# Sliding-window attention with two MLPs: sinks inside each key tile, and one value tile shared by both query blocks of a unit

## The chip, the cores and the metric

The kernel runs on one core of a Trainium2 chip. The metric is the device time of one execution in microseconds (us). The engines are PE (TensorE; its weight loads are listed apart as PEld), DVE (VectorE), ACT (ScalarE), POOL (GpSimd) and SP, which here only issues DMAs.

## The reference: what is computed

```python
def _attn_ref(q, k, v, n_sink, window):            # q, k, v: [2, 8, 768, 64]
    scores = (1 / sqrt(64)) * (q @ k^T)
    keep = (pos_k < n_sink) | (0 <= pos_q - pos_k < window)     # n_sink 4, window 128
    scores = where(keep, scores, -1e9); a = exp(scores - max); a = a / (sum(a) + 1e-9)
    return a @ v
x = attention, heads side by side                   # [1536, 512]
x = elu(x @ w_in) @ w_out                           # [512, 2048], [2048, 512]
x = prelu(x @ w2_in, alpha) @ w2_out                # the same sizes
```

All inputs and the output are float32.

## The kernel before

**Attention.** A *unit* is the work of four heads on 128 queries: two head pairs (e = 0, 1), each of two heads (f = 0, 1). There are 24 units, x0 to x23 by the number of their output tile. Four of them (p = 0) hold the first 128 positions and have less work. The 128 queries of a unit are two blocks of 64 (j = 0, 1). Block 0 sees 128 keys of the tile before and the first 64 of its own; block 1 sees the last 64 of the tile before and all 128 of its own. Each also sees six sink columns, which the launch copies between the tiles, so a row of scores is 198 wide (`WMAX` = 128 + 6 + 64).

A unit passes these stages, each on one line of the code:

- `qk` (L766): eight score products on PE, K = 64 rows, 198 columns;
- `s` (L781): mask and row maximum on DVE; `s` (L789): exp and row sum on ACT; `st` (L799, L800): one over the sum on DVE; `s` (L817): the scaling on POOL;
- `t` (L837): sixteen transposes on PE; `pt` (L852): two copies out of PSUM, each on ACT or DVE as the planner chooses;
- `x` (L879): the value products on PE. For a unit with p > 0 each block has a full tile of 128 keys (kind "t") and an edge tile of 64 keys and 6 sinks (kind "e"), so 2 blocks x 2 tiles x 2 pairs x 2 heads = 16 products of 64 columns;
- `xh` (L893) on ACT and `xl` (L898) on DVE: the result split in a high and a low part.

Both full tiles differ: block 0 uses the 128 keys before the unit, block 1 the unit's own 128.

**MLPs.** Every product is done as three fp32r products of 128x128 weights with 512 columns (high x high, high x low, low x high), all on L983. `h` tiles are the first layer, `o` tiles the second; h0_0_3 is round 0, tokens 0 to 511, chunk 3. A *group* is the three products of one 128-row slice; four groups fill one h or o tile. Weights come as raw words and are decoded in eight steps on ACT, DVE and POOL (L438 to L460). An h tile goes through ACT (L1004, L1011), DVE (L1016), a copy `gh` on ACT or POOL (L1024) and a subtraction `gl` on DVE or POOL (L1027) before an o tile can use it.

**Order.** A planner (`class Plan`) places every step on an engine's queue with costs that are written in the code (800 ns for the `x` step of a unit with p > 0), and the engines then run these queues in order. Where it sees PE idle for more than 700 ns, it writes products that nobody reads into the queue (`busy`, L422), one for each 128 ns over that. `BANKS` lets at most three MLP tiles be open in PSUM in the planner's books. Loads of keys and values lie in one field of SBUF (`acc`, `more`), and a load is placed where the units that used that space have given it back.

Of the kernel before, what the change touches and what calls it, by code (L numbers as in the profile page):

```python
# [15 lines left out]
AF = mybir.ActivationFunctionType  # L16
# [3 lines left out]
B, H, S, D = 2, 8, 768, 64  # L20
NT, DM, DFF = B * S, H * D, 2048
P = 128
# [6 lines left out]


WIN, SINK, QB = 128, 6, 64
NPAIR = S // P
HP = H // 2

# [40 lines left out]
def key_columns(lo, hi):  # L75

    cols, scored = [], {}
    if lo:  # L80
        cols += range(lo * P - P, lo * P)
    for p in range(lo, hi):
        n = len(cols)
        if p:
            cols += [-1 - i for i in range(SINK)]
            scored[p] = (n - P, P + SINK + QB), (n - QB, QB + SINK + P)
        else:
            scored[p] = (0, QB), (0, P)
        cols += range(p * P, p * P + P)
    return cols, scored  # L90


# [8 lines left out]
SPAN, NCH, CR, VTILE, _cols = [], [], [], {}, []  # L101
for _r, (_lo, _hi) in enumerate(VRANGE):
    _sinks = [-1 - i for i in range(SINK)]
    _edge = [c for p in range(max(_lo, 1), _hi) for c in (*range(p * P - QB, p * P), *_sinks, *_sinks, *range(p * P, p * P + QB))]
    for _kind, _more, _high in (("t", [*range(_lo * P, _hi * P)], P), ("e", _edge, QB + SINK)):
        if _more:
            VTILE[_kind, _r] = len(SPAN), sum(NCH) * 2 * D, len(_more) // _high
            SPAN.append((len(_cols), len(_more)))
            NCH.append(len(_more) // _high)
            CR.append(_high)  # L110
            _cols += _more
KCOLS.append(_cols)
WMAX = P + SINK + QB
KTOT = [len(c) for c in KCOLS]

RUNS = [
    [(0, QB, 0)], [(0, P, -QB)], [(0, P, -P), (P, SINK, None), (P + SINK, QB, 0)],
    [(0, P, -P), (P, SINK, None), (P + SINK, QB, 0)], [(0, QB, -P), (QB, SINK, None), (QB + SINK, P, -QB)],  # L120
]
SINKS = [0, 0, 0, P, QB]
MW = [c + n for c, n, _ in (runs[-1] for runs in RUNS)]


def mask_of(p, j):
# [167 lines left out]
def attention_mlp2(  # L294
# [13 lines left out]
    nc = tc.nc  # L308
# [45 lines left out]
    def v_of(kind, b, hp, p):  # L354
        r = next(r for r, (lo, hi) in enumerate(VRANGE) if lo <= p < hi)
        return (kind, b, r, hp), p - (VRANGE[r][0] if kind == "t" else max(VRANGE[r][0], 1))
# [33 lines left out]
    for i, most in enumerate((SINK, 0, WIN, 0)):  # L390
# [7 lines left out]
        out=flag_i, in0=int1[:, 2:3].bitcast(U32), scalar=0.5, in1=flag_m, op0=ALU.is_ge, op1=ALU.mult  # L398
# [245 lines left out]
    for m in range(2):  # L644
        o = FIRST + sum(MW[:m])
# [5 lines left out]
    def fast_path():  # L651
# [35 lines left out]
        needs_v, first_v = {}, {}  # L687
        for i, (g, p) in enumerate(units):
            b, z, hp = sgs[g]
            needs_v[i] = [v_of("t", b, hp, p)[0]] + ([v_of("t", b, hp, p - 1)[0], v_of("e", b, hp, p)[0]] if p else [])  # L690
            for v in needs_v[i]:
                first_v.setdefault(v, i)
        uses_v = {v: sum(x.count(v) for x in needs_v.values()) for v in first_v}
# [55 lines left out]
        for i, (g, p) in enumerate(units):  # L749
            b, z, hp = sgs[g]  # L750
            nk, nq = KTOT[z], QTOT[z]
            tiles = {}
# [23 lines left out]
            for j, (_, w) in enumerate(SCORED[z][p]):  # L776
                m = mask_of(p, j)
                for e in range(2):

                    def least(e_, tiles=tiles, j=j, e=e, w=w, m=m):  # L780
                        nc.vector.tensor_tensor_reduce(  # L781
                            out=tiles["s"][:, j, e, :w], in0=tiles["qk", e][:, j * WMAX : j * WMAX + w],
                            in1=masks[m], scale=-SCALE, scalar=3.0e38, op0=ALU.add, op1=ALU.min,
                            accum_out=tiles["st"][:, 0, j, e : e + 1],
                        )

                    def power(e_, tiles=tiles, j=j, e=e, w=w):
                        s, st = tiles["s"], tiles["st"]
                        nc.scalar.activation(  # L789
                            s[:, j, e, :w], s[:, j, e, :w], AF.Exp, bias=st[:, 0, j, e : e + 1], scale=-1.0,  # L790
                            accum_out=st[:, 1, j, e : e + 1],
                        )

                    op = plan.add({"DVE": 75.0 + 1.06 * w}, least, deps=[sc, ready[m]], frees=[hq[e]], rank=i)
                    exps.append(plan.add({"ACT": 290.0 + 0.8 * w}, power, deps=[op], rank=i))

            def shares(e_, tiles=tiles):
# [7 lines left out]

            parts = (
                [[(1, 0, 0, QB)], [(0, 1, 0, P)]] if p == 0 else
                [[(0, 0, 0, P), (1, 0, P, QB + SINK)], [(1, 1, 0, QB + SINK), (0, 1, QB + SINK, P)]]
            )
            high_ = [P, QB if p == 0 else QB + SINK]  # L810
            ns_ = []
            for j, (_, w) in enumerate(SCORED[z][p]):
                for e in range(2):

                    def normal(e_, tiles=tiles, j=j, e=e, w=w):
                        s, st = tiles["s"], tiles["st"]
                        nc.gpsimd.tensor_scalar(  # L817
                            out=s[:, j, e, :w], in0=s[:, j, e, :w], scalar1=st[:, 3, j, e : e + 1], scalar2=1.0,
                            op0=ALU.mult, op1=ALU.mult,
                        )  # L820

                    ns_.append(plan.add({"POOL": 250.0 + 0.8 * w}, normal, deps=[share], rank=i, lock=True))


            def turned(e_, i=i, p=p, tiles=tiles, ht=ht, parts=parts):
                s = tiles["s"].rearrange("p j e w -> p (j e w)")
                for f in range(2):
                    tiles["t", f] = bank(f"t{i}_{f}", ht[f].slot)
                for j in range(2):
                    for a, _, c0, r in parts[j]:  # L830
                        r = min(r, QB) if p == 0 and a else P
                        for e in range(2):
                            o = (a * 4 + j * 2 + e) * QB
                            for f in range(2):
                                at_ = slice(f * QB, f * QB + QB)
                                r0 = (j * 2 + e) * WMAX + c0
                                nc.tensor.transpose(tiles["t", f][:r, o : o + QB], s[at_, r0 : r0 + r], ident[at_, at_])  # L837

            turns = plan.add(
# [7 lines left out]
            for f in range(2):  # L847
# [6 lines left out]
                n = sum(hi - lo for _, lo, hi in cuts_)  # L854
# [4 lines left out]
            def values(e_, i=i, p=p, b=b, hp=hp, tiles=tiles, hx=hx):  # L859
                px = tiles["x"] = bank(f"x{i}", hx.slot)  # L860

                def v(kind, p, n=0):
                    key, at_ = v_of(kind, b, hp, p)
                    return tiles_v[key][:, :, at_ * (1 if kind == "t" else 2) + n]

                if p == 0:
                    uses_ = [[(1, v("t", 0), QB)], [(0, v("t", 0), P)]]
                else:
                    uses_ = [
                        [(0, v("t", p - 1), P), (1, v("e", p, 1), QB + SINK)],  # L870
                        [(1, v("e", p), QB + SINK), (0, v("t", p), P)],
                    ]
                for j in range(2):
                    for e in range(2):
                        o = (e * 2 + j) * QB
                        for n, (a, vt, r) in enumerate(uses_[j]):
                            q0 = (a * 4 + j * 2 + e) * QB
                            for f in range(2):
                                nc.tensor.matmul(  # L879
                                    px[f * D : f * D + D, o : o + QB], vt[:r, e, f * D : f * D + D],  # L880
                                    tiles["p", f][:r, q0 : q0 + QB],
                                    start=(n == 0), stop=(n == len(uses_[j]) - 1),
                                )

            va = taken[i] = plan.add(
                {"PE": sum(len(x) for x in parts) * 4 * 50.0}, values,
                deps=copied + [land_v[v] for v in needs_v[i]],
                takes=[(kinds["tx"], 1, hx)], frees=hv + [hold_v[v] for v in needs_v[i]], rank=i - 3.0, kind="v",
            )
            c0, o = b * S + p * P, 2 * P  # L890
# [62 lines left out]
        for n, (kind, k, t, x) in enumerate(PIECES):  # L953
            m, r = divmod(k, NR)
            c0, nt = TOK[t]
            rank, op, hold, tiles = 100.0 + n, None, Hold(2 if kind == "f" else 1), {}
            for j in range(FG):
                if kind == "f":
                    w, half = split[k, 0, x]
# [272 lines left out]
```

## Time and profile before

| | |
|---|---|
| median of 3 runs | 612.57 us (610.41 to 613.4) |
| the profiled execution | 609.28 us |
| its span, first to last instruction | 607.50 us, granted clock 0.998 |
| PE / PEld / DVE / ACT / POOL busy | 596.2 / 493.7 / 439.6 / 294.8 / 85.1 us |
| chain that ended last | PE 96%, DVE 1%, issue 1%, ACT 1% |
| of it by line | h and o (L983) 86%, x (L879) 4%, qk (L766) 3%, t (L837) 2%, busy (L422) 2% |
| DMA | 50.92 MB, 17.62 MB of it in the first 100 us on the queue of the loads |

The profiled execution took 609.28 us, 1.78 us more than its span. Attention fills the first 82 us of the span, with four groups of MLP between its last units; after that PE runs MLP products to the end. Busy shares over the whole span hide that: ACT is busy for 49% of the span, but for 19.11 of the 20 us from 40 to 60. "issue" in a chain or a wait is time in which an engine waited for nothing that the profile shows.

### The profile page before, as it was taken

The page shows a single profiled execution, that of the slowest core. Times are in us where ns is not written, and L with a number is a line of the kernel's source. Part 1 is how long each engine was busy: PE and PEld are TensorE (multiplying, and loading weights), DVE is VectorE, ACT ScalarE, POOL GpSimd, SP SyncE. Part 2 cuts the span into 40 slices and gives each one's busy share as a digit, 9 for nine tenths or more (in the row PEclk, how much of TensorE's full clock was granted, in tenths as well). Part 3 has the DMA queues.
Part 4 walks back from the last instruction along what each step waited for, and adds up shares of the span by engine and source line. Part 5 has one row for each costly group of instructions (what it writes and reads, how often), then busy time and mean ns, then how long its engine had stood idle before and what let it go on. Part 6 is the DMA issues. An engine that isn't in the chain of part 4 may idle for free.

```text
span 607.5 us, 10062 instructions
## 1 busy us (share of the span) xinstructions
PE 596.2 (98%) x3832; PEld 493.7 (81%) x3832; DVE 439.6 (72%) x930; ACT 294.8 (49%) x642; POOL 85.1 (14%) x175
## 2 busy tenths in 40 slices
PE   8989999999999999999999999999999999999996
PEld 7877878888888888888888888888888888888885
DVE  5788889999988667575848796966778774455452
ACT  5989998677747444634655253536142321011010
POOL 5555520101011000200045120000000000000000
PEclk9999999999999999999999999999999999999999
DMA  8987133354431212130402112222202000000112
GB/s 236 285 249 229 42 105 112 98 165 147 138 105 44 97 38 101 35 105 0 140 1 75 64 53 87 70 71 69 70 35 70 1 1 0 1 0 1 69 54 91
DMA packets 19251, 50.92 MB, mean 84 GB/s; under 512 B 2154, under 2 KB 6810, under 8 KB 19194
## 3 DMA queue, kind: packets, MB, share of 16 engines
q1 hardware_dynamic: 18744, 49.92, 26.4%
q8 instruction: 32, 0.52, 0.4%
q10 hardware_dynamic: 450, 0.27, 0.2%
q14 instruction: 25, 0.20, 0.1%
HBM read 47.04 MB, written 3.15 MB: 83 GB/s over the span
## 4 chain that ended last, share of the span: by engine, by line
PE 96%; DVE 1%; issue 1%; ACT 1%; POOL 0%; ACTq 0%; POOLq 0%; DVEq 0%
PE h L983 43%; PE o L983 43%; PE x L879 4%; PE qk L766 3%; PE t L837 2%; PE busy L422 2%; DVE s L781 1%; ACT s L789 0%; ACT pt L852 0%; DVE pt L852 0%; DVE xl L898 0%; ACT xh L893 0%; DVE acc L1049 0%; DVE st L800 0%; DVE st L799 0%
## 5 line engine op out<-in xcount | busy, mean ns | idle before, releaser
L983 PE MATMUL h<-xh,wh 128*128 128x512 f32 x384 | 149.9, 390 | 0.0
L983 PE MATMUL o<-gl,wh 128*128 128x512 f32 x384 | 149.4, 389 | 0.0
L983 PE MATMUL h<-xh,wl 128*128 128x512 f32 x384 | 149.4, 389 | 0.0
L983 PE MATMUL h<-xl,wh 128*128 128x512 f32 x384 | 149.4, 389 | 0.0
L983 PE MATMUL o<-gh,wh 128*128 128x512 f32 x384 | 149.4, 389 | 0.0
L983 PE MATMUL o<-gh,wl 128*128 128x512 f32 x384 | 149.4, 389 | 0.0
L1024 ACT CAST gh<-u 128x512 fp32r<-128x512 f32 x88 | 54.6, 620 | 161.6 <-DVE u L1018 142.0
L1027 DVE TENSOR_TENSOR gl<-u,gh 128x512 fp32r<-128x512 f32 x91 | 63.3, 696 | 35.7 <-ACT gh L1024 33.0
L1049 DVE TENSOR_TENSOR acc<-o,acc 128x512 f32<-128x512 f32 x72 | 49.0, 687 | 49.3 <-PE o L983 49.3
L983 PEld LDWEIGHTS o<-gl,wh 128*128 128x128 f32 x384 | 72.1, 188 | 15.1 <-DVE gl L1027 0.2
L983 PEld LDWEIGHTS h<-xh,wl 128*128 128x128 f32 x384 | 72.1, 188 | 15.1
L983 PEld LDWEIGHTS h<-xh,wh 128*128 128x128 f32 x384 | 72.1, 188 | 15.1
L983 PEld LDWEIGHTS o<-gh,wl 128*128 128x128 f32 x384 | 72.1, 188 | 15.0
L983 PEld LDWEIGHTS o<-gh,wh 128*128 128x128 f32 x384 | 72.1, 188 | 15.0
L983 PEld LDWEIGHTS h<-xl,wh 128*128 128x128 f32 x384 | 72.1, 188 | 14.8
L460 DVE TENSOR_TENSOR wl<-wx,wh 128x512 fp32r<-128x512 f32 x64 | 45.8, 718 | 19.1 <-POOL wh L458 9.6
L438 ACT ACTIVATE wx<-wr 128x512 f32<-128x512 f32 x64 | 43.1, 674 | 31.9 <-DVE wl L460 31.9
L458 POOL CAST wh<-wx 128x512 fp32r<-128x512 f32 x21 | 13.4, 637 | 272.0 <-DVE wl L460 161.2
L1006 DVE TENSOR_SCALAR u<-h,alpha_sb 128x512 f32<-128x512 f32 x48 | 35.8, 746 | 21.4 <-PE h L983 21.4
L454 DVE CUSTOM_DVE_ANT_0 wx<-wx,wq 128x1024 uint16<-128x1024 uint16 x64 | 46.0, 719 | 2.6
L458 ACT CAST wh<-wx 128x512 fp32r<-128x512 f32 x43 | 26.7, 621 | 40.5 <-PE h L983 18.1
L450 DVE SCALAR_TENSOR_TENSOR wx<-wr,wx 128x512 int32<-128x512 int32 x64 | 44.7, 698 | 1.3
(56 smaller groups left out, 623.2 us busy)
## 6 DMA issues: line engine op xcount, KB each, us to landing
wr<-in_w_dram SPq DMA_DIRECT2D x64, 512.0 KB, 3.5
out_dram<-acc SPq DMA_DIRECT2D x12, 256.0 KB, 2.3
more<-in_kq_dram SPq DMA_DIRECT2D x3, 914.0 KB
more<-in_kq_dram SPq DMA_DIRECT2D x3, 652.0 KB, 7.7
more<-in_vc_dram SPq DMA_DIRECT2D x6, 280.0 KB
acc<-in_vc_dram SPq DMA_DIRECT2D x8, 128.0 KB, 6.0
acc<-in_vc_dram SPq DMA_DIRECT2D x4, 256.0 KB, 12.2
more<-in_vc_dram SPq DMA_DIRECT2D x4, 256.0 KB, 8.5
```

The lines of the kernel that those rows point to most:

```text
L438: nc.scalar.activation(xf, high.bitcast(F32), AF.Abs)
L450: nc.vector.scalar_tensor_tensor(out=x, in0=high, scalar=-0x40000000, in1=x, op0=ALU.bitwise_and, op1=ALU.bitwise_or)
L454: nc.vector.tensor_tensor(out=x, in0=x, in1=r, op=ALU.add)
L458: (nc.gpsimd.tensor_copy if eng == "POOL" else nc.scalar.copy)(wh, xf)
L460: nc.vector.tensor_tensor(out=wl, in0=xf, in1=wh, op=ALU.subtract)
L766: nc.tensor.matmul(tiles["qk", e][f * QB : f * QB + QB, j * WMAX : j * WMAX + w], k[:, q : q + QB], k[:, f * nk + k0 : f * nk + k0 + w], s ...
L879: nc.tensor.matmul(px[f * D : f * D + D, o : o + QB], vt[:r, e, f * D : f * D + D], tiles["p", f][:r, q0 : q0 + QB], start=(n == 0), stop= ...
L983: nc.tensor.matmul(tiles["p"][:, :nt], lhs[:, cols], rhs, start=(j == 0 and q == 0), stop=(j == FG - 1 and q == 2),)
L1006: nc.vector.tensor_scalar(out=u, in0=hp, scalar1=0.0, scalar2=alpha_sb[:, fc : fc + 1], op0=ALU.min, op1=ALU.mult)
L1024: (nc.gpsimd.tensor_copy if e == "POOL" else nc.scalar.copy)(src["h"], tiles["u"])
L1027: (nc.gpsimd if e == "POOL" else nc.vector).tensor_tensor(out=src["l"], in0=tiles["u"], in1=src["h"], op=ALU.subtract)
L1049: nc.vector.tensor_tensor(out=a, in0=po, in1=a, op=ALU.add)
```

## The change

The sinks move from between the key tiles to the middle of each: a tile is now its first 64 keys, six sinks, its last 64 keys. Both blocks' rows stay 198 wide. The 128 keys from 64 before the unit's first position to 63 after it lie in the rows of both blocks. They become the full value tile of the unit, which both blocks share. Each block keeps an edge tile of 64 keys and 6 sinks, at the outer end of its row.

So per pair and head there is one product of 128 columns (both blocks) and one of 64 for each block: 12 products in a unit with p > 0 in place of 16. `place` lays the transposed blocks of a pair side by side so that one product can read both; the two blocks of a unit swap places in the tile `s`. A unit no longer uses the full tile of the range before it (`needs_v` loses an entry). Each key load of a unit with p > 0 gains six columns per head, 6 KB for a load. The planner's cost of the `x` step goes from 800 to 820 ns (400 to 450 for p = 0). The masks' column runs follow the new order.

```diff
-    _edge = [c for p in range(max(_lo, 1), _hi) for c in (*range(p * P - QB, p * P), *_sinks, *_sinks, *range(p * P, p * P + QB))]
+    _edge = [c for p in range(max(_lo, 1), _hi) for c in (*range(p * P - P, p * P - QB), *_sinks, *_sinks, *range(p * P + QB, p * P + P))]
+    _main = range(_lo * P - QB, _hi * P - QB) if _lo else range(P)
...
+        cols += [*range(p * P, p * P + QB), *(-1 - i for i in range(SINK)), *range(p * P + QB, p * P + P)]
+        if p >= lo:
+            scored[p] = (n - P - SINK, WMAX), (n - QB, WMAX)
...
+def place(p, a, j, e):
+    return (a * 4 + (e * 2 + j if p else j * 2 + e)) * QB
...
-            needs_v[i] = [v_of("t", b, hp, p)[0]] + ([v_of("t", b, hp, p - 1)[0], v_of("e", b, hp, p)[0]] if p else [])
+            needs_v[i] = [v_of("t", b, hp, p)[0]] + ([v_of("e", b, hp, p)[0]] if p else [])
...
-                        [(0, v("t", p - 1), P), (1, v("e", p, 1), QB + SINK)],
-                        [(1, v("e", p), QB + SINK), (0, v("t", p), P)],
+                        (0, 0, P, v("t", p), P, 0), (0, 1, QB, v("e", p), QB + SINK, 2),
+                        (1, 1, QB, v("e", p, 1), QB + SINK, 3),
...
-                for j in range(2):
-                    for e in range(2):
+                for e in range(2):
+                    for j, a, n, vt, r, state in uses_:
...
-                {"PE": sum(len(x) for x in parts) * 4 * 50.0}, values,
+                {"PE": 820.0 if p else 450.0}, values,
```

What this does to PE's queue is shown at two places. The first is the value products of unit 6 (`x6` is its output in PSUM, `pt6_0` and `pt6_1` its transposed probabilities by head, `acc` and `more` the fields that hold the values). Before, its sixteen products begin:

```order
L879 MATMUL x6_729<-pt6_0_701,acc_70 64x64
L879 MATMUL x6_729<-pt6_1_703,acc_70 64x64
L879 MATMUL x6_729<-pt6_0_701,more_161 64x64
L879 MATMUL x6_729<-pt6_1_703,more_161 64x64
L879 MATMUL x6_729<-pt6_0_701,acc_70 64x64
L879 MATMUL x6_729<-pt6_1_703,acc_70 64x64
L879 MATMUL x6_729<-pt6_0_701,more_161 64x64
L879 MATMUL x6_729<-pt6_1_703,more_161 64x64
```

After the change the whole of unit 6 is these twelve:

```order
L880 MATMUL x6_715<-pt6_0_686,more_161 64x128
L880 MATMUL x6_715<-pt6_1_690,more_161 64x128
L880 MATMUL x6_715<-pt6_0_686,more_161 64x64
L880 MATMUL x6_715<-pt6_1_690,more_161 64x64
L880 MATMUL x6_715<-pt6_0_686,more_161 64x64
L880 MATMUL x6_715<-pt6_1_690,more_161 64x64
L880 MATMUL x6_715<-pt6_0_686,more_161 64x128
L880 MATMUL x6_715<-pt6_1_690,more_161 64x128
L880 MATMUL x6_715<-pt6_0_686,more_161 64x64
L880 MATMUL x6_715<-pt6_1_690,more_161 64x64
L880 MATMUL x6_715<-pt6_0_686,more_161 64x64
L880 MATMUL x6_715<-pt6_1_690,more_161 64x64
```

Four products of 128 columns stand in for eight of 64, and all of the unit's values now lie in `more`, since the range before (in `acc`) is not used. The same holds for each of the 20 units with p > 0.

The second place is in the first round of the MLP, where the first group of the tile h0_0_3 stands. Before, it stands among groups of h0_0_2 and h0_2_1:

```order
L983 MATMUL h0_2_1_1988<-xh_123,wh0_1_0_1848 128x512
L983 MATMUL h0_2_1_1988<-xl_124,wh0_1_0_1848 128x512
L983 MATMUL h0_2_1_1988<-xh_123,wl0_1_0_1849 128x512
L983 MATMUL h0_0_2_2013<-xh_123,wh0_2_0_1903 128x512
L983 MATMUL h0_0_2_2013<-xl_124,wh0_2_0_1903 128x512
L983 MATMUL h0_0_2_2013<-xh_123,wl0_2_0_1904 128x512
L983 MATMUL h0_0_3_2047<-xh_123,wh0_3_0_1944 128x512
L983 MATMUL h0_0_3_2047<-xl_124,wh0_3_0_1944 128x512
L983 MATMUL h0_0_3_2047<-xh_123,wl0_3_0_1945 128x512
```

Now the last group of h0_1_2, a `busy` stretch and the first group of o0_0_0 surround it:

```order
L983 MATMUL h0_1_2_1949<-xh_123,wh0_2_0_1820 128x512
L983 MATMUL h0_1_2_1949<-xl_124,wh0_2_0_1820 128x512
L983 MATMUL h0_1_2_1949<-xh_123,wl0_2_0_1821 128x512
L424 MATMUL busy6_1999<-ident_101 128x128 x4
L983 MATMUL h0_0_3_2004<-xh_123,wh0_3_0_1872 128x512
L983 MATMUL h0_0_3_2004<-xl_124,wh0_3_0_1872 128x512
L983 MATMUL h0_0_3_2004<-xh_123,wl0_3_0_1873 128x512
L983 MATMUL o0_0_0_2012<-gh0_0_0_1834,wh0_0_1_1924 128x512
L983 MATMUL o0_0_0_2012<-gl0_0_0_1835,wh0_0_1_1924 128x512
L983 MATMUL o0_0_0_2012<-gh0_0_0_1834,wl0_0_1_1925 128x512
```

The planner sees a hole of PE before h0_0_3, which it did not see anywhere after attention before; and o0_0_0 starts as soon as h0_0_3 does. The `busy` products before the last value product go from 44 to 36 in all: the stretches of 10, 2 and 7 at the start stay, those ahead of unit 4's transposes and of its value products go from 11 and 1 to 3 and 4, the 3 ahead of unit 14 stay, and the 4 and 6 around unit 20 become one stretch of 7. Six MLP groups stand ahead of the last value product where four stood. On ACT, DVE and POOL the same work stands in slightly other order: ACT has 22 large copies `pt` where it had 21, and DVE 18 where it had 19. SP's DMAs keep their order.

## Rows read from the trace of the kernel before

**Rows 1.** Busy time by stretch: us, busy (instructions) by engine, clock, DMA.

```profile
40.00:60.00 20.00, 19.24 (x456) 15.87 (x453) 17.39 (x89) 19.11 (x75) 11.72 (x28) 1.00 0.79 235
60.00:80.00 20.00, 19.38 (x401) 16.09 (x402) 16.69 (x65) 18.31 (x60) 10.32 (x24) 1.00 0.13 41
80.00:180.00 100.00, 100.00 (x480) 82.55 (x475) 93.47 (x165) 74.00 (x130) 10.50 (x15) 1.00 0.42 132
```

**Rows 2.** Chain that ended last, 28 to 36: start us, us, what.

```profile
29.11 0.83 PE qk L766 x16
...
30.59 0.38 PE x L879 x6
30.96 2.00 issue
32.96 1.98 PE x L879 x58
```

**Rows 3.** The same chain, 57 to 66.

```profile
59.28 0.33 PE t L837 x6
59.61 1.00 issue
60.62 0.52 PE t L837 x10
61.14 1.08 PE x L879 x32
```

**Rows 4.** Busy time and instructions between and far behind the two stalls.

```profile
31.20:59.50 28.30, 26.12 (x630) 21.80 (x631) 23.19 (x115) 24.99 (x96) 16.22 (x39) 1.00 0.82 241
200.00:400.00 200.00, 200.00 (x884) 165.60 (x883) 144.56 (x237) 98.36 (x166) 25.57 (x24) 1.00 0.21 69
```

**Rows 5.** DMA queues in 200 to 400: packets, MB, share.

```profile
q8 instruction: 7, 0.11, 0.2%
```

**Rows 6.** DMA queues in 30 to 32.

```profile
q1 hardware_dynamic: 363, 0.43, 99.0%
q8 instruction: 1, 0.02, 3.9%
```

**Rows 7.** Timeline of ACT, 31 to 62, and what ended idle time.

```profile
34.02 0.37 ACT L893 CAST xh<-x 128x256 fp32r<-128x256 f32 x1 [2.26 <-PE x L879]
...
61.19 0.59 ACT L852 COPY pt<-t 128x512 f32<-128x512 f32 x1 [0.67 <-PE t L837]
```

**Rows 8.** Timeline of PE around 63.4: start, us, line, form, count.

```profile
63.27 0.29 PE L879 MATMUL x<-pt,acc 128*64 128x64 f32 x4
63.38 0.40 PE L879 MATMUL x<-pt,more 70*64 70x64 f32 x8
```

**Rows 9.** The chain again, 66 to 90.

```profile
69.89 1.09 PE busy L422 x8
...
72.06 1.53 PE busy L422 x12
...
80.36 0.90 PE h L983 x3
...
82.34 7.71 PE h L983 x33
```

**Rows 10.** Groups by form, 82 to 106: count, busy us, mean ns.

```profile
L1011 ACT ACTIVATE u<-u 128x512 f32<-128x512 f32 x8 | 5.1, 633 | 0.2
L1016 DVE SCALAR_TENSOR_TENSOR u<-u,h 128x512 f32<-128x512 f32 x7 | 4.8, 683 | 0.3 <-ACT u L1011 0.2
...
L1004 ACT ACTIVATE u<-h 128x512 f32<-128x512 f32 x7 | 4.1, 589 | 0.6 <-PE h L983 0.6
...
L1027 DVE TENSOR_TENSOR gl<-u,gh 128x512 fp32r<-128x512 f32 x5 | 3.5, 709 | 0.9 <-ACT gh L1024 0.9
```

**Rows 11.** POOL groups by form, whole span.

```profile
L1024 POOL CAST gh<-u 128x512 fp32r<-128x512 f32 x8 | 5.4, 681 | 36.5 <-DVE u L1016 27.2 <-PE o L983 9.3
```

More of the change, by code (lines that the diff above doesn't have):

```diff
@@ L31 @@
 WIN, SINK, QB = 128, 6, 64
+WMAX = P + SINK + QB
 NPAIR = S // P
@@ L79, in key_columns @@
     cols, scored = [], {}
-    if lo:
-        cols += range(lo * P - P, lo * P)
-    for p in range(lo, hi):
+    if not lo:
+        return [*range(P)], {0: ((0, QB), (0, P))}
+    for p in range(lo - 1, hi):
         n = len(cols)
[L84 to L89, printed above, removed]
+        cols += [*range(p * P, p * P + QB), *(-1 - i for i in range(SINK)), *range(p * P + QB, p * P + P)]
+        if p >= lo:
+            scored[p] = (n - P - SINK, WMAX), (n - QB, WMAX)
     return cols, scored
@@ L103 @@
     _sinks = [-1 - i for i in range(SINK)]
-    _edge = [c for p in range(max(_lo, 1), _hi) for c in (*range(p * P - QB, p * P), *_sinks, *_sinks, *range(p * P, p * P + QB))]
-    for _kind, _more, _high in (("t", [*range(_lo * P, _hi * P)], P), ("e", _edge, QB + SINK)):
+    _edge = [c for p in range(max(_lo, 1), _hi) for c in (*range(p * P - P, p * P - QB), *_sinks, *_sinks, *range(p * P + QB, p * P + P))]
+    _main = range(_lo * P - QB, _hi * P - QB) if _lo else range(P)
+    for _kind, _more, _high in (("t", [*_main], P), ("e", _edge, QB + SINK)):
         if _more:
@@ L112 @@
 KCOLS.append(_cols)
-WMAX = P + SINK + QB
 KTOT = [len(c) for c in KCOLS]
 RUNS = [
-    [(0, QB, 0)], [(0, P, -QB)], [(0, P, -P), (P, SINK, None), (P + SINK, QB, 0)],
-    [(0, P, -P), (P, SINK, None), (P + SINK, QB, 0)], [(0, QB, -P), (QB, SINK, None), (QB + SINK, P, -QB)],
+    [(0, QB, 0)], [(0, P, -QB)], [(0, QB, -P), (QB, SINK, None), (QB + SINK, P, -QB)],
+    [(0, QB, -P), (QB, SINK, None), (QB + SINK, P, -QB)], [(0, P, -P), (P, SINK, None), (P + SINK, QB, 0)],
 ]
-SINKS = [0, 0, 0, P, QB]
+SINKS = [0, 0, 0, QB, P]
 MW = [c + n for c, n, _ in (runs[-1] for runs in RUNS)]
+def place(p, a, j, e):
+    return (a * 4 + (e * 2 + j if p else j * 2 + e)) * QB
 def mask_of(p, j):
@@ L781, in least @@
                         nc.vector.tensor_tensor_reduce(
-                            out=tiles["s"][:, j, e, :w], in0=tiles["qk", e][:, j * WMAX : j * WMAX + w],
+                            out=tiles["s"][:, 1 - j, e, :w], in0=tiles["qk", e][:, j * WMAX : j * WMAX + w],
                             in1=masks[m], scale=-SCALE, scalar=3.0e38, op0=ALU.add, op1=ALU.min,
@@ L789, in power @@
                         nc.scalar.activation(
-                            s[:, j, e, :w], s[:, j, e, :w], AF.Exp, bias=st[:, 0, j, e : e + 1], scale=-1.0,
+                            s[:, 1 - j, e, :w], s[:, 1 - j, e, :w], AF.Exp, bias=st[:, 0, j, e : e + 1], scale=-1.0,
                             accum_out=st[:, 1, j, e : e + 1],
@@ L807, in fast_path @@
                 [[(1, 0, 0, QB)], [(0, 1, 0, P)]] if p == 0 else
-                [[(0, 0, 0, P), (1, 0, P, QB + SINK)], [(1, 1, 0, QB + SINK), (0, 1, QB + SINK, P)]]
+                [[(1, 0, 0, QB + SINK), (0, 0, QB + SINK, P)], [(0, 1, 0, P), (1, 1, P, QB + SINK)]]
             )
@@ L817, in normal @@
                         nc.gpsimd.tensor_scalar(
-                            out=s[:, j, e, :w], in0=s[:, j, e, :w], scalar1=st[:, 3, j, e : e + 1], scalar2=1.0,
+                            out=s[:, 1 - j, e, :w], in0=s[:, 1 - j, e, :w], scalar1=st[:, 3, j, e : e + 1], scalar2=1.0,
                             op0=ALU.mult, op1=ALU.mult,
@@ L832, in turned @@
                         for e in range(2):
-                            o = (a * 4 + j * 2 + e) * QB
+                            o = place(p, a, j, e)
                             for f in range(2):
                                 at_ = slice(f * QB, f * QB + QB)
-                                r0 = (j * 2 + e) * WMAX + c0
+                                r0 = ((1 - j) * 2 + e) * WMAX + c0
                                 nc.tensor.transpose(tiles["t", f][:r, o : o + QB], s[at_, r0 : r0 + r], ident[at_, at_])
@@ L866, in values @@
                 if p == 0:
-                    uses_ = [[(1, v("t", 0), QB)], [(0, v("t", 0), P)]]
+                    uses_ = [(0, 0, QB, v("t", 0), QB, 1), (1, 0, QB, v("t", 0), P, 1)]
                 else:
                     uses_ = [
-                        [(0, v("t", p - 1), P), (1, v("e", p, 1), QB + SINK)],
-                        [(1, v("e", p), QB + SINK), (0, v("t", p), P)],
-                    ]
-                for j in range(2):
-                    for e in range(2):
+                        (0, 0, P, v("t", p), P, 0), (0, 1, QB, v("e", p), QB + SINK, 2),
+                        (1, 1, QB, v("e", p, 1), QB + SINK, 3),
+                    ]
+                for e in range(2):
+                    for j, a, n, vt, r, state in uses_:
                         o = (e * 2 + j) * QB
[L876 to L883, printed above, removed]
+                        q0 = place(p, 1 - j if p == 0 else a, j, e)
+                        for f in range(2):
+                            nc.tensor.matmul(
+                                px[f * D : f * D + D, o : o + n], vt[:r, e, f * D : f * D + D],
+                                tiles["p", f][:r, q0 : q0 + n], start=state < 2, stop=state % 2 == 1,
+                            )
             va = taken[i] = plan.add(
-                {"PE": sum(len(x) for x in parts) * 4 * 50.0}, values,
+                {"PE": 820.0 if p else 450.0}, values,
                 deps=copied + [land_v[v] for v in needs_v[i]],
```

## The prediction

> **What bounds the kernel now.** I read the busy time by stretch first. From 80 us on PE is busy all the time, 100.00 of 100 us, while DVE has 93.47 [rows 1]. So after attention the end moves only with what PE runs, and with a wait that DVE might cause there. From 40 to 60 us ACT has 19.11 of 20 us, PE 19.24 and DVE 17.39 [rows 1]: in the middle of attention ACT is as full as PE, so a shorter PE step alone brings little there. Time can come from places where these engines stand still, and I looked for those in the chain of waits.
>
> There are two. At 30.96 us PE stops for 2.00 us in the value products of unit 6, after three of the sixteen (six records; each float32 product leaves two) [rows 2]. At 59.61 us it stops for 1.00 us inside the transposes of unit 17 [rows 3]. The profile names no releaser in either case ("issue"). Both stops reach ACT: it waits 2.26 us for the value products until 34.02, and 0.67 us for the transposes until 61.19 [rows 7].
>
> I take both for waits for instructions. Between them lie 630 PE and 631 PEld records, 1261 [rows 4]. In the quiet stretch from 200 to 400 us PE and PEld have 884 + 883 = 1767 [rows 4], and the instruction queue q8 has 7 packets of together 0.11 MB [rows 5]: 252 instructions for a packet. 1261 / 252 = 5.0, so the two stops are five packets apart, up to the few waits that are instructions without a row here. And in 30 to 32 us the queue of the data has 99.0% of the 16 engines, with one instruction packet among it [rows 6]. So a block of some 256 instructions came late because it stood behind the loads of keys and values.
>
> The Trainium skill ("Runtime: NRT & Kernel Launch", section "Instruction fetch mechanics") also has blocks of 256 instructions, but calls the crossing mostly hidden. Its block size agrees with the 252 here; its second statement doesn't agree with the 2.00 and 1.00 us. By that statement there would be no such stop to remove, and my sum below would lack its largest terms; that is the second rival.
>
> **The change part by part.** The value products: each of 20 units goes from 16 products of 64 columns to 4 of 128 and 8 of 64, with the same 1024 columns. Two products that belong to the two heads run side by side: such a pair starts 0.11 us after the one before (63.27 to 63.38) [rows 8], eight pairs take 1.08 us with their start [rows 3]. No row shows a pair of 128 columns with all 128 rows. It costs at least the 0.11 us of a narrow pair, which would save 2 x 0.11 = 0.22 us in a unit, 4.4 us in 20. At most I give it the rate of the score products: eight products of 198 columns, four side by side, take 0.83 us [rows 2], 0.415 us for 198 columns with the start, so 0.27 us for 128; that would lose 2 x 0.05 = 0.10 us in a unit, 2.0 us in 20. I take 0.22 us, twice the narrow pair: 1.7 ns a column there against 2.1 in the score products says that columns and not the number of products set the time. This term is 0. Only the last five units, behind the last score products, run where nothing but PE bounds them, so the ends that count are -1.1 and +0.5 us.
>
> By the Trainium skill ("TensorE: Matmul & The Clock Gate", sections "The mechanism" and "LDWEIGHTS (loading the stationary operand)") a weight load overlaps with a running product only in other rows of the array, and 64 columns of weights take 64 / 1.2 = 53 ns. All value products use the same rows, so by that rule the loads of the four products that go are bare time; an estimate from that page is 8 loads, two side by side, 0.21 us a unit. The row speaks against it: two such loads alone would fill the 0.11 us from pair to pair [rows 8] and leave nothing for the products.
>
> The first stop. The loads ahead of the packet stay as they are: 6 KB more in each of eight key loads are 48 KB, 0.2 us at 241 GB/s [rows 4], and no wait of PE for a load is on the chain. So I leave the block's arrival at 32.96 us. What PE has done by then changes. Up to unit 6 the queue is shorter by 5 `busy` products (12 to 7) and by four products in each of units 4 and 5, 13 products, which count four instructions each (two loads, two products): 52. So the boundary lies 52 instructions later, 64 into unit 6's value products: behind all twelve (48) and four products of unit 7. Before, 29 products of units 6 and 7 were left when the block came, 1.98 us [rows 2]; now eight, 8 / 29 x 1.98 = 0.55 us. Unit 7's products end some 1.4 us earlier if the block comes at the same time, less if its later request delays it: 52 instructions are about a third of a microsecond of such work. ACT has unit 6's result out of the way meanwhile, but still waits for unit 7's. I take 0.8 us, with 0 and 2.00 as the ends. The five `busy` products that go before that, 1.3 us, gain nothing of their own, since PE runs into the block sooner for them. ACT is full behind this place, so that what it gains there stays gained.
>
> The second stop. A unit has 112 instructions where it had 128 (8 score products of four, 16 transposes of two, 16 value products of four), so a block lasts 256 / 112 = 2.3 units in place of 2. Ten more units (6 to 15) move the boundaries by another 160, so that this one comes at the end of the score products of unit 22, when most loads have landed: from 60 to 80 us DMA's share is 0.13 where it was 0.79 [rows 1]. I expect no stop of note there. It cost ACT 0.67 and PE 1.00 us; I take 0.8, with 0 and 1.0 as the ends.
>
> The `busy` products: four of them take 1.09 us and six 1.53 [rows 9], some 0.27 each. Around unit 20, where PE is the only bound, 7 stand for 10: -0.8 us. In the MLP's first round 4 are new: +1.1 us, and nothing hides them, since PE is full there. The planner put them there because its books allow three open MLP tiles; the chip has no such limit, so PE doesn't wait on top of them. Together +0.3 us. The two groups that moved ahead of the last value product are the same work at another place, 0.
>
> The first round's feed. o0_0_0 now stands close behind h0_0_3. Its last group needs gl of h0_0_3, and between lie one o group and four groups of h0_1_3. Eleven groups take 7.71 us [rows 9], 0.70 each, so the cover is 3.5 us. The way of the tile is 589 + 633 on ACT, 683 on DVE, 681 on POOL and 709 on DVE [rows 10, 11]: 3.30 us without hand-overs and queues. It is covered by a hair. I take +0.3 us; the ends are 0 and four DVE instructions of 683 ns in front of it, 2.7 us.
>
> **The sum.** 0 - 0.8 - 0.8 + 0.3 + 0.3 = -1.0 us. The profiled execution took 609.28 us (span 607.50 and 1.78 around it), so 608.3 for one like it. It is 3.3 us under the median of the runs shown, 612.57, which is what I predict from: 611.6 us.
>
> **The rivals.** *More than forecast.* Both stops go whole, 3.0 us, the loads of the last five units were bare after all, 1.1 us, and the feed never waits: -3.0 - 1.1 + 0.3 = -3.8, 608.8 us. For it: PE and ACT are both near full in attention, so a saved microsecond has no other brake. Against it: the boundary only moves past unit 6, and 0.11 us a pair leaves no room for bare loads.
>
> *The stops only move.* Blocks still come late, in unit 7 and then in another unit, or the two stops had another cause, such as a wait that the profile doesn't show: 0 + 0.3 + 0.3 = +0.6, 613.2 us. For it: the first one's arrival hangs on loads that stay. Against it: units use 16 instructions fewer for each 128.
>
> *DVE doesn't keep up.* Slower than before: DVE has 6.5 us of air in the 100 us behind attention [rows 1]. PE comes there 1.6 us sooner, with two more groups behind it, and the plan has o tiles right behind the h tiles that feed them. If gl comes 2.7 us late for o0_0_0 and again for the next o tile, the waits are 5.4: -1.6 + 0.3 + 5.4 = +4.1, 616.7 us. It decides once such waits pass 1.3 us in all. For it: the planner itself saw a hole there. Against it: before, PE never waited there, and only one place has so little cover.
>
> **How the numbers follow.** The forecast has 0.57, more than forecast 0.17, the stops only move 0.18, DVE 0.08. A measurement of this kernel tells about 0.5%, 3.06 us, from no change. Faster than 609.5 are most of the first rival (0.15) and the forecast's edge (0.04): 0.19. Slower than 615.6 are the third rival and little else: 0.08. Within: 0.73. The range reaches from just below the first rival's 608.8 to beyond the second's 613.2 with a part of the feed's 2.7: 608.4 to 614.6.
>
> **What would show it.** Right: in the chain of the changed kernel the "issue" of 2.00 us in unit 6 becomes one of about 1.5 in unit 7, and no "issue" near 1.00 us is left around 60 us; the twelve value products of a unit take 1.03 to 1.08 us; the last one ends 1.5 to 3 us before 82.34; one stretch of four `busy` products stands in the MLP, with a wait of at most 0.5 us for gl after it. Wrong: value products of a unit at 0.9 us or less (bare loads), stops of the same size in other units (the second rival), or idle PE of more than a microsecond between 80 and 180 us (the third).

## The result and the profile after

| | before | after |
|---|---|---|
| median, runs taken together | 610.51 us (608.13 to 613.75, 20 runs) | 613.87 us (610.76 to 616.52, 20 runs) |
| span of the profiled execution | 607.5 us | 611.8 us |
| PE / DVE busy | 596.2 / 439.6 us | 597.4 / 437.9 us |

The ratio is 1.0057, with a 95% interval of 1.0042 to 1.0072: the change makes the kernel slower by some 3.5 us.

To see where the profiled executions part, I counted the MLP products (L983) and compared the start of the nth in both traces, each from the first `busy` product. Every kernel runs 2304 of them. The trace of the kernel before is of an execution of 609.28 us, 1.2 us under the median of its twenty runs, so such a lag can be that much larger than the medians tell.

| nth MLP product | what lies before it | after behind before, us |
|---|---|---|
| 20 to 95 | attention, then MLP with the same pace | 0.66 |
| 105 | four `busy` products | 1.57 |
| 120 | first wait for gl | 4.03 |
| 150 to 2303 | a second, short one | 4.25 |

So 0.66 us come from attention, 0.91 from the `busy` products and 2.68 from the feed; behind that no time is lost or won for the rest of the kernel. The first of these is the least firm. Three kernels below give PE the same queue through attention as the kernel after has, and their attention ends 0.00, 0.56 and 0.80 us behind that of the kernel before.

The chain that ended last in the kernel after shows attention's stops (start us, us, what):

```profile
30.39 1.60 PE x L880 x31
31.99 1.58 issue
33.58 0.79 PE x L880 x13
...
39.55 0.86 PE x L880 x6
40.41 1.15 issue
41.56 0.84 PE x L880 x17
...
64.43 0.83 PE qk L768 x15
65.25 1.37 issue
66.62 0.38 PE qk L768
...
71.37 1.76 PE busy L424 x14
...
83.31 1.06 PE x L880 x24
84.36 5.68 PE h L983 x24
```

Two stops of 2.00 and 1.00 us [rows 2, 3] became three, of 1.58 us in unit 7, 1.15 in unit 9 and 1.37 in the score products of unit 22, 4.10 us in all. The last value product ends at 84.36 us where it was 82.34 [rows 9], with six MLP groups done in place of four. Two groups are 1.4 us, so attention itself is some 0.6 us late.

Busy time by stretch, the rows that answer to [rows 1]:

```profile
40.00:60.00 20.00, 18.85 (x392) 15.68 (x396) 15.78 (x82) 18.03 (x70) 11.43 (x29) 1.00 0.64 184
60.00:80.00 20.00, 18.63 (x326) 15.20 (x316) 15.46 (x66) 18.01 (x62) 11.32 (x27) 1.00 0.33 80
80.00:180.00 100.00, 97.86 (x484) 80.26 (x484) 94.05 (x166) 73.96 (x130) 13.99 (x18) 1.00 0.43 132
```

PE is idle for 2.14 us between 80 and 180 us, where it never was. And from 60 to 80 us the transfers have a share of 0.33 where it was 0.13: the loads run later than before. The waits of PE, by what it waited for (us in total, times, longest), name both places:

```profile
PE x L880 <- issue: 2.7, 2, 1.6
PE o L983 <- DVE gl L1027: 2.1, 1, 2.1
...
PE qk L768 <- issue: 1.4, 1, 1.4
```

The timeline of PE has that wait in o0_0_0 (start us, us, instruction, idle before it and releaser):

```profile
107.10 0.39 PE L983 MATMUL o<-gh,wh 128*128 128x512 f32 x1
109.63 0.50 PE L983 MATMUL o<-gl,wh 128*128 128x512 f32 x1 [2.14 <-DVE gl L1027]
```

By the order of the program this is its third group, which needs gl of h0_0_2. ACT has that tile's copy gh ready at 106.47 (105.87 and 0.60 in its row), yet DVE makes gl only at the end of the last row below. Its timeline, and the row of ACT's copy:

```profile
105.24 0.77 DVE L462 TENSOR_TENSOR wl<-wx,wh 128x512 fp32r<-128x512 f32 x1
105.94 0.41 DVE L444 TENSOR_SCALAR wx<-wx 128x512 f32<-128x512 f32 x1
106.39 0.43 DVE L448 TENSOR_SCALAR wx<-wx 128x512 int32<-128x512 int32 x1
106.85 0.69 DVE L452 SCALAR_TENSOR_TENSOR wx<-wr,wx 128x512 int32<-128x512 int32 x1
107.68 0.69 DVE L456 CUSTOM_DVE_ANT_0 wx<-wx,wq 128x1024 uint16<-128x1024 uint16 x1
108.29 1.28 DVE L1027 TENSOR_TENSOR gl<-u,gh 128x512 fp32r<-128x512 f32 x2
```

```profile
105.87 0.60 ACT L1024 CAST gh<-u 128x512 fp32r<-128x512 f32 x1
```

Steps that decode a later weight tile, 2.2 us, and gl of another h tile stand ahead of it in DVE's queue. DVE runs its queue in order and is idle for at most 0.14 us at a time between these rows. So 3.1 us pass from the end of gh to the end of gl, of which gl itself takes 0.7.

### The profile page after: what moved, and what is told of

Read it like the earlier page. It is cut to its first block, busy times and chain, and to the rows that moved or that the text cites. A ratio compares the mean times of both kernels' runs of the same rounds, so it can differ in the third digit from the quotient of the medians.

```text
span 611.8 us, 9732 instructions
## 1 busy us (share of the span) xinstructions
PE 597.4 (98%) x3664; PEld 492.9 (81%) x3664; DVE 437.9 (72%) x927; ACT 295.9 (48%) x643; POOL 89.7 (15%) x177
## 4 chain that ended last, share of the span: by engine, by line
PE 94%; DVE 2%; ACT 1%; DMA 1%; issue 1%; ACTq 0%; DVEq 0%
PE o L983 43%; PE h L983 40%; PE x L880 4%; PE qk L768 3%; PE t L839 2%; PE busy L424 1%; DMA acc<-in_kq_dram 1%; DMA ints<-in_limits_dram 0%; ACT u L1004 0%; DVE gl L1027 0%; ACT u L1011 0%; ACT wx L440 0%; DVE wl L462 0%; ACT wq L442 0%; DVE wx L452 0%
## 5 line engine op out<-in xcount | busy, mean ns | idle before, releaser
L983 PE MATMUL o<-gl,wh 128*128 128x512 f32 x384 | 149.7, 390 | 2.1 <-DVE gl L1027 2.1
L983 PE MATMUL h<-xh,wh 128*128 128x512 f32 x384 | 150.1, 391 | 0.0
L983 PE MATMUL h<-xh,wl 128*128 128x512 f32 x384 | 149.5, 389 | 0.0
L983 PE MATMUL h<-xl,wh 128*128 128x512 f32 x384 | 149.5, 389 | 0.0
L983 PE MATMUL o<-gh,wl 128*128 128x512 f32 x384 | 149.5, 389 | 0.0
L983 PE MATMUL o<-gh,wh 128*128 128x512 f32 x384 | 149.4, 389 | 0.0
L983 PEld LDWEIGHTS o<-gl,wh 128*128 128x128 f32 x384 | 72.1, 188 | 17.8 <-DVE gl L1027 2.9
L983 PEld LDWEIGHTS h<-xh,wh 128*128 128x128 f32 x384 | 72.1, 188 | 15.1
L983 PEld LDWEIGHTS h<-xh,wl 128*128 128x128 f32 x384 | 72.1, 188 | 15.1
L983 PEld LDWEIGHTS o<-gh,wl 128*128 128x128 f32 x384 | 72.1, 188 | 15.0
L983 PEld LDWEIGHTS o<-gh,wh 128*128 128x128 f32 x384 | 72.1, 188 | 14.9
L983 PEld LDWEIGHTS h<-xl,wh 128*128 128x128 f32 x384 | 72.1, 188 | 14.7
L1027 DVE TENSOR_TENSOR gl<-u,gh 128x512 fp32r<-128x512 f32 x87 | 60.4, 697 | 30.4 <-ACT gh L1024 27.4
L1004 ACT ACTIVATE u<-h 128x512 f32<-128x512 f32 x48 | 28.5, 593 | 33.2 <-PE h L983 33.0
```

The costliest lines, as they stand in the source:

```text
L983: nc.tensor.matmul(tiles["p"][:, :nt], lhs[:, cols], rhs, start=(j == 0 and q == 0), stop=(j == FG - 1 and q == 2),)
L1004: nc.scalar.activation(u, hp, AF.Relu, scale=-1.0)
L1027: (nc.gpsimd if e == "POOL" else nc.vector).tensor_tensor(out=src["l"], in0=tiles["u"], in1=src["h"], op=ALU.subtract)
```

## The experiments

All ratios are against runs of the kernel before on the same chip in the same batch. The first three ask whether the order of the first MLP round costs the time, or the new products do.

**Hold o0_0_0 back** until h0_1_3 is done, in the kernel after:

```diff
-                    op_.behind(lasts[n - 2])
+                    op_.behind(lasts[n - 2 + (n == 10)])
```

> The changed kernel, but the tile o0_0_0 may start only when h0_1_3 is done (one line of the planner); all else of PE's queue up to there, the four busy products included, stays. Feed theory (o0_0_0 stands too close behind what DVE must deliver for it, which cost 2.46 + 0.22 us): the waits of PE for gl vanish, 2.7 us less than the changed kernel, so about 0.7 us in attention and 0.9 for the busy products over the kernel before: ratio to before near 1.0025. Rival (DVE is the bound of the whole first round, and PE waits for it wherever the o tiles stand): the wait comes again at a later product, and the time stays within 0.5 us of the changed kernel, ratio near 1.0057.

Measured: 0.9989 (0.9966 to 1.0011), median 611.03 against 611.38. The wait for gl has shrunk to this (timeline of PE):

```profile
112.65 0.50 PE L983 MATMUL o<-gl,wh 128*128 128x512 f32 x1 [0.38 <-DVE gl L1027]
```

The lag at the end is 1.56 us, of it 0.91 for the `busy` products, which this kernel keeps. All the new value products are in it, and the slowdown is gone: the order, not the products. The forecast of 1.0025 lies above the interval. Like the 1.56 us it rests on the profile of the kernel before, which is of an execution 2.1 us under the median of this batch.

**The old cost in the planner**, 800 and 400 ns for a unit's value products, in the kernel after:

```diff
-                {"PE": 820.0 if p else 450.0}, values,
+                {"PE": 800.0 if p else 400.0}, values,
```

> The changed kernel with the planner's old costs of the value step (800 and 400 ns in place of 820 and 450). The products are the same twelve, but the planner writes another order: h0_0_3, h0_1_2 and h0_1_3 whole ahead of o0_0_0, four busy products still in the MLP. Feed theory: no wait for gl over 0.5 us, 2.7 us less than the changed kernel, ratio to before 1.001 to 1.004, the rest from where the block boundaries fall in attention. If the loss were in the new products or the loads themselves, the ratio would stay at 1.0057.

Measured: 1.0027 (1.0006 to 1.0047), median 612.16. The planner now puts o0_0_0 behind h0_1_2 and h0_1_3, and in the MLP the lag grows by 2.17 us in place of 3.59; one wait of 0.85 us for a gl, made on POOL, is left, where none over 0.5 us was forecast. By the ratio about half of the loss is left, by the interval a tenth to four fifths of it, so the rest came through that one number. It also changes the order in attention, which ends 1.13 us sooner here than in the kernel after, so this run alone doesn't tell how much of that is the first round's.

**The order alone**: the kernel before with its sixteen products and a cost of 760 ns, at which the planner writes the order of the kernel after in the first round.

```diff
-                {"PE": sum(len(x) for x in parts) * 4 * 50.0}, values,
+                {"PE": 760.0 if p else 400.0}, values,
```

> The kernel before with its 16 value products untouched; only the planner's cost of a unit's value products is 760 in place of 800 ns. With that the planner writes the MLP's first round in the changed kernel's order: the first group of o0_0_0 stands between the groups of h0_0_3, and five busy products ahead of it. Feed theory (the order costs the time, whatever the products): PE waits 2 us or more for gl at a group of o0_0_0 and runs the five busy products, 1.3 us; ratio to the kernel before 1.003 to 1.007. Rival (the new products cost the time): no wait for gl over 0.5 us, ratio 0.998 to 1.002.

Measured: 1.0053 (1.0029 to 1.0077), median 614.46 against 610.74, as much as the whole change. The wait is there with the old products, a little under the 2 us forecast:

```profile
112.17 0.50 PE L983 MATMUL o<-gl,wh 128*128 128x512 f32 x1 [1.78 <-DVE gl L1027]
```

In the MLP the lag grows by 3.48 us (1.14 `busy`, 2.34 feed), as 3.59 in the kernel after. In the profiled execution attention was 3.3 us late as well, with a stop of 2.14 us at 60.58 and a granted clock of 0.78 behind it, so that profile, of 616.14 us, is longer than the median tells. The cost changes the order in attention too; that the loss is in the first round is read from the 3.48 us.

The next three ask what sets that stretch: PE with its `busy` products, or DVE. **No `busy` products in the MLP**, kernel after:

```diff
-            if got and got[0] < t:
+            if got and got[0] < t and not later:
```

> The changed kernel without the four busy products in the MLP; PE's queue is otherwise the same. If DVE sets the moment at which o0_0_0 goes on (feed theory), PE comes there 0.9 us sooner and waits 0.9 us longer: the wait for gl is about 3.2 us in place of 2.3 and the MLP behind it ends at the same time, 0.0 us gained. If the busy products add to the wait (the sum of the prediction), the wait stays 2.1 to 2.3 us and the MLP ends 0.9 us sooner.

Measured, in a single execution: 614.91 us, no gain but a lag of 5.56 us at the end, 4.76 of it in the MLP. The 0.9 us come off and waits take them: o0_0_0 goes on at 109.79 us where it was 109.63, behind two waits in place of one (timeline of PE, then busy time by stretch; the clock is the third figure from the right):

```profile
106.77 0.47 PE L983 MATMUL o<-gh,wh 128*128 128x512 f32 x1 [0.28 <-ACT gh L1024]
109.79 0.80 PE L983 MATMUL o<-gl,wh 128*128 128x512 f32 x1 [2.54 <-DVE gl L1027]
110.38 0.63 PE L983 MATMUL o<-gh,wl 128*128 128x512 f32 x1
```

```profile
105.00:110.00 5.00, 2.18 (x9) 1.31 (x8) 4.79 (x9) 4.08 (x8) 0.61 (x1) 0.95 0.35 116
110.00:115.00 5.00, 5.00 (x17) 3.96 (x18) 4.71 (x9) 1.90 (x4) 1.21 (x2) 0.71 0.15 58
```

Products start 0.23 us apart where PE doesn't wait. By that pace the two starts come 3.2 us late in sum, where the one in the kernel after is 2.3 us late: the 0.9 us that were forecast. Behind the wait the products take 0.63 us where they take 0.39 elsewhere: the granted clock is at the lower level, 1.2 GHz, for a part of these 5 us. So in the kernel after the four `busy` products stand in time that PE would have waited anyway. That nothing is gained was forecast; the lower clock, which makes it 1.2 us worse than the kernel after, was not.

**Both, held back and without `busy`:**

> The changed kernel with o0_0_0 held back until h0_1_3 is done, and no busy products in the MLP. If PE sets that stretch, the 0.9 us of the four busy products come off: from 150 products on it lies 0.9 us ahead of the version with o0_0_0 held back alone, waits for gl stay at 0.6 us, ratio to the kernel before about 0.997. If DVE sets it, the waits for gl grow by the same 0.9 to about 1.5 us, nothing is gained, ratio about 0.999.

Measured: 1.0004 (0.9986 to 1.0023). The lag in the MLP grows by 1.54 us; with `busy` products it was 1.56. The 0.91 us saved came back as waits of o groups. The second is for DVE; the first is for a copy on POOL, which waits for DVE itself (timelines of PE and POOL):

```profile
110.81 1.21 POOL L1024 CAST gh<-u 128x512 fp32r<-128x512 f32 x2 [5.43 <-DVE u L1016]
112.07 0.50 PE L983 MATMUL o<-gh,wh 128*128 128x512 f32 x1 [0.39 <-POOL gh L1024]
113.22 0.50 PE L983 MATMUL o<-gl,wh 128*128 128x512 f32 x1 [0.64 <-DVE gl L1027]
```

In this order DVE sets this stretch, as the second of the two theories had it.

**The measured decode costs in the planner**, without `busy` in the MLP:

```diff
-                {"ACT": 560.0}, {"ACT": 570.0}, {"DVE": 336.0}, {"DVE": 336.0}, {"DVE": 609.0}, {"DVE": 602.0},
+                {"ACT": 560.0}, {"ACT": 570.0}, {"DVE": 455.0}, {"DVE": 455.0}, {"DVE": 727.0}, {"DVE": 610.0},
```

> The changed kernel with the planner's costs of the four decode steps on DVE set to what the trace shows (455, 455, 727, 610 ns in place of 336, 336, 609, 602), and no busy products in the MLP. The planner then puts o0_0_0 behind most of h0_1_3 by itself. If the low costs in the planner's books are the root of the early o0_0_0, the waits for gl are under 0.5 us in all, ratio about 0.997. If DVE's work as a whole sets the stretch, waits of 1 us or more remain in whatever order, ratio 0.999 to 1.001.

Measured: 1.0004 (0.9981 to 1.0027), median 610.96. The waits for gl are gone, 0.14 us of lag in the whole MLP. That half of the forecast held: it was the order, since DVE has the same work. The ratio did not reach 0.997, and why the twelve runs miss it is not shown. The profile is of the longest of them, 612.97 us: attention is 3.42 us late there, behind a stop of 2.13 us at 32.78. Busy time by stretch:

```profile
30.00:35.00 5.00, 2.87 (x67) 2.35 (x60) 2.92 (x15) 3.34 (x12) 1.96 (x5) 0.98 1.07 273
35.00:40.00 5.00, 5.00 (x63) 3.58 (x63) 2.44 (x11) 2.76 (x11) 1.19 (x3) 0.50 1.01 250
40.00:45.00 5.00, 5.00 (x90) 3.95 (x84) 3.75 (x23) 3.77 (x16) 2.25 (x7) 0.84 0.56 193
```

From 35 to 40 us PE ran at 1.2 GHz throughout.

The last five ask what the stops are. **Six warming products in place of ten** in the kernel before; four `busy` products fewer are 16 instructions, 8 PE records:

```diff
-NWARM = 10
+NWARM = 6
```

> The kernel before with 6 in place of 10 busy products at the very start: 16 PE instructions fewer ahead of all that follows, nothing else. Instruction block theory: the stop of 2.00 us in unit 6 moves four products on, from behind the third to behind the seventh of its value products (14 records in place of 6), and the one of 1.00 us in unit 17's transposes moves eight transposes on, near the end of that unit's sixteen; their lengths stay about the same, and the time within 0.5 us. Rival (a wait for data or an engine that the profile doesn't name): both stops stay at their product.

Measured: 0.9991 (0.9967 to 1.0015). The chain:

```profile
31.81 0.61 PE x L879 x14
32.42 1.22 issue
33.63 1.74 PE x L879 x50
...
59.48 0.58 PE t L837 x11
60.07 0.15 issue
```

The first stop stands after 14 records of unit 6 where it stood after 6 [rows 2], exactly 8 on, and lasts 1.22 us. The second moved as well and is 0.15 us: in the timeline it stands behind fourteen of unit 17's sixteen transposes, where it stood behind six (the chain lists fewer of them). The places are those forecast; the lengths, which were to stay, are not. Nothing that these instructions compute was touched; only their number ahead changed. A wait for data would have stayed at its record. The other profiles say the same: counted from the start of the kernel, the stop near 32 us stands behind 468 or 469 PE records in all thirteen, each one near 40 us behind 595, and each one from 60 to 69 us behind 1096 to 1099, whatever product that is.

**Held back, without `busy`, six warming products:**

> As the version with o0_0_0 held back and no busy products in the MLP, with 6 warming products at the start in place of 10: 16 PE instructions fewer ahead of attention. If the stops without a releaser are blocks of instructions that come late, each one stands eight PE records further on (in unit 7 behind about 15 records in place of 7, in unit 9 eight on as well, in the score products of unit 22 eight on), and together they are 0.5 to 1.5 us shorter; PE starts unit 0 about 1.2 us later. If they are waits for loads or for another engine, they stay at their record. Ratio to the kernel before 0.995 to 0.999 against 0.997 to 1.000.

Measured: 0.9989 (0.9966 to 1.0012). The stops of 1.59, 1.18 and 1.16 us with ten are 0.81 and 0.99 us with six, each eight records further on, as forecast. Of the third 0.12 us is left, in the value products behind. Attention ends 1.25 us sooner. The ratios of the two don't part.

**Measured decode costs, no `busy` in the MLP, and 6, 2 or 14 warming products:**

> The version with the measured decode costs in the planner and no busy products in the MLP, with 6 warming products at the start in place of 10, so 16 PE instructions fewer ahead of attention. Theory (blocks of instructions come late, and a stop of over 2 us costs granted clock behind it): the stop in unit 7 stands 16 instructions further on and is 0.5 to 1 us shorter than the 2.13 us of the version with 10; no stretch of the profile falls under a granted clock of 0.95; waits for gl stay under 0.5 us; ratio to the kernel before 0.995 to 0.999. Rival (stops and warming products don't matter): ratio 1.000 to 1.001 as with 10.

> The same with 2 warming products: 32 PE instructions fewer ahead of attention than with 10. Theory: the stop in unit 7 stands 32 instructions further on than with 10 and is 1 to 2 us shorter; against it PE starts attention with fewer warming products, at most 1.2 us later for each four taken away; ratio to the kernel before 0.994 to 0.999. Rival: ratio 1.000 to 1.003, the later start and nothing else.

> The same with 14 warming products: 16 PE instructions more ahead of attention than with 10. Theory: the stop stands 16 instructions earlier, in unit 6's last products or unit 7's first, and is longer, 2.3 us or more; the granted clock falls behind it in the profile or in more of the runs; ratio to the kernel before 1.001 to 1.006. Rival: ratio 1.000 to 1.001 as with 10.

| warming products | ratio | stops of over 0.5 us, in order | lowest clock of a 5 us stretch, 15 to 80 us |
|---|---|---|---|
| 14 | 0.9995 (0.9969 to 1.0021) | 1.95, 1.69, 1.43 | 0.80 |
| 10 | 1.0004 (0.9981 to 1.0027) | 2.13, 0.63 | 0.50 |
| 6 | 0.9988 (0.9965 to 1.0010) | 0.90, 0.70 | 1.00 |
| 2 | 0.9981 (0.9959 to 1.0002) | 0.82, 1.03 | 1.00 |

With six the chain has:

```profile
31.23 1.94 PE x L880 x36
33.16 0.90 issue
34.07 0.45 PE x L880 x7
...
39.71 1.14 PE x L880 x11
40.85 0.70 issue
```

The stops move and shrink as forecast with six and two. With 14 the first stands eight records sooner, as forecast, but was to be 2.3 us or more and the ratio at least 1.001; it was 1.95 us, and the ratio went with the rival. The intervals of all four overlap, and each holds the rival's 1.000: the traces tell the theory from the rival, the times don't. The lowest ratio, with two warming products, comes with a median of 610.08 us against 611.11: no version here beats the kernel before beyond doubt.

## Why the prediction was wrong

It forecast 611.6 us and a change too small to tell; the kernel became slower by 0.57%. In the profiled executions it said -1.0 us and the lag is +4.25. Of these 5.25 us attention makes 3.06 (-2.4 forecast, two stops and the `busy` products around unit 20; +0.66 measured), the feed 2.38, and the `busy` products in the MLP -0.19. The median of 613.87 us lies inside 608.4 to 614.6 all the same, which is luck: the forecast started from three runs with a median of 612.57, and the twenty have 610.51. Two of its own signs of being wrong are there, stops of the same size in other units and 2.14 us of idle PE behind attention.

**The first round's feed failed**, as the term that was mis-sized: "It is covered by a hair. I take +0.3 us; the ends are 0 and four DVE instructions of 683 ns in front of it, 2.7 us." It measured 2.68 us, the far end. The cover of PE groups was weighed against 3.30 us "without hand-overs and queues", and the queue was the point: four decode steps stand ahead of gl on DVE. It was also taken for another tile, gl of h0_0_3 for the last group; the third group's gl of h0_0_2 came late first. Holding o0_0_0 back takes the loss away with the new products in place, the order alone makes it with the old ones, and the measured decode costs in the planner end it (there without `busy` products). The planner puts the first two decode steps at 336 ns; they take 0.41 and 0.43 us in the rows above. That such numbers are the root is borne out by the last of these only, which changed the order as a whole.

**The stops did not go.** The forecast gave -0.8 for each; attention as a whole came out at +0.66, although the `busy` products around unit 20 came off as forecast (1.76 us in the chain for 2.62 [rows 9]). The first block boundary was where the prediction put it, in unit 7 after four of its products, and so was the later one, in the score products of unit 22. Three things were wrong.

First, "I leave the block's arrival at 32.96 us": PE went on at 33.58, 0.62 us later, and unit 7's products end at 34.36 where they ended at 34.93 [rows 2], 0.57 us sooner, for a term of 0.8. The prediction did ask what a later request would cost, but put 52 instructions at "about a third of a microsecond"; they are thirteen products, 0.9 us by its own 1.98 us for 29. Second, unit 22's stop was taken for harmless because "most loads have landed"; the loads ran later in the kernel after, and it cost 1.37 us. Third, the boundary between, in unit 9, was not looked at; PE had crossed it without a stop before. By the trace's instruction packets, the block for that boundary landed at 35.38 us before and at 40.30 us after. The packet took 1.3 us in either case; it began 1.14 us after PE had gone on at the boundary ahead of it before, and 5.47 us after.

In all three stops of the kernel after PE goes on 1.26 to 1.44 us behind the end of a packet (32.14 to 33.58, 40.30 to 41.56, 65.24 to 66.62), and 1.48 and 1.54 us behind it in the two before (31.48 to 32.96, 59.08 to 60.62). That they are late blocks is shown by the kernels with fewer warming products; that they are late because of the loads ahead of them is argued only, from the full queue [rows 6] and shares of 0.98, 1.01 and 0.91 in the kernel after from 25 to 30, 35 to 40 and 60 to 65 us, ahead of its three stops. No run took loads away. The Trainium skill ("Runtime: NRT & Kernel Launch", section "Instruction fetch mechanics") calls such crossings mostly hidden; the 1.15 to 1.58 us here speak against it for this stretch.

**Value products: 0, right.** Twelve take 1.06 us in the chain above, sixteen took 1.08 [rows 3].

**`busy` products: +0.3, about right in price.** The four in the MLP cost 0.91 us where 1.1 was forecast. But "nothing hides them" was wrong: without them PE waits for DVE for as long.

**The rivals.** What happened is the second and the third together: the stops only moved, and DVE did not keep up, by 2.68 us where that rival had 5.4. It was given 0.08 because PE had never waited there; but the order was new.

## What to carry over

A product that waits for a short chain on another engine is covered only if the whole queue of that engine ahead of the chain's last step is counted, not the chain alone. A change in one number of a planner moves work far from the edit: compare the orders, and time the new order with the old code. Where PE is full but the end does not move when its work is taken away, look for the engine that it would wait for next.

## What was not expected of the hardware

After a stop of some 2 us the granted clock fell to the lower level, 1.2 GHz, in four profiles: behind 2.54 us (0.71 from 110 to 115), 2.13 (0.50 from 35 to 40), 2.14 (0.78 from 60 to 65, 0.87 from 65 to 70), and 1.69, some 6 us behind another of 1.95 (0.86 and 0.80 from 40 to 50). It did not behind 2.00 us in the kernel before nor behind 2.14 in the kernel after, so the length of the stop alone doesn't decide. What it cost can be estimated from the granted clock, as the part missing to 1.00 over the stretches around: 3.4 us behind the stop of 2.13, which is more than the stop, and some 1.7 us in each of the others.

Of the runs with six or two warming products 38 of 48 have a mean granted clock of 0.998 or more; with ten, it is 21 of 93 in the kernel before and 18 of 60 in five of the kernels above. With 14 it is 6 of 12, so shorter stops are not the whole of it, and what else sets this stays open.
